# Two of four 768-column differences of token operands made by GpSimd (Pool) instead of VectorE

## The chip, the cores and the metric

One core of a Trainium2 chip runs the whole program. The metric is the time of one execution on the device, in microseconds (us); lower is better. The time of the kernel before is the median of three runs; the profile is that of one execution, which has its own time.

## What is computed

An attention with 32 memory slots, a feed-forward layer with a clipped gate, and a mixture of four experts, all in float32:

```python
a = softmax(phi)                                  # (b, h, s, m), over s
k_m, v_m = a^T k, a^T v                           # 32 memory rows per head
attn_out = softmax(q k_m^T / sqrt(64)) v_m
x = attn_out as (2304, 512)
h = x @ w_in                                      # 2048 columns
x = (h * clip(h + 3, 0, 6) / 6) @ w_out
p = domain_probs / sum(domain_probs)
out = sum over e of p[:, e] * (relu(x @ w1[e]) @ w2[e])   # e = 0..3, 1024 columns each
```

## The kernel before

Every matmul operand is split into a high part (a cast by ScalarE, ACT in the profile) and a low part (a difference by VectorE, DVE), and TensorE (PE) runs three matmuls per product: high by high, high by low, low by high.

**First part.** Attention and the gated layer for 6 token tiles of 384 columns. Their instructions are put in order by a planner at build time (class `Plan`), from written costs and dependences; x^T comes out as the tiles `acc`, one per token tile, as four blocks of 384 columns.

**Second part.** The experts, in 3 passes (p = 0, 1, 2) over pairs of token tiles. A pass has 8 steps n (expert and half of its columns). A step has two units (`unit`), and then the second matmul of the layer (`second`, L953) for both token tiles: 6 blocks of 128 tokens, each added up by DVE into `oacc` (L961, or L959 at the first step of a pass). A unit does a 2 by 2 block product with seven block products instead of eight (L897, banks `pb`, `pa`, `pc`, `pd`): its weight operands `W` are made from `u_raw` by four additions or differences on Pool (`s1`, `s3`, `s2`, `s4`, L326 to L335), a cast on ACT (L320) and a low part on DVE (L323). Products in a unit go b, a, c, d, a, c, d. The second `a` goes into the bank that the first filled, so it waits until DVE has read the first into `u2` (L905, tile `u`), which in turn needs ACT's copy `p6` of bank b (L914, tile `p`).

**The token operands.** The seven blocks that the units multiply by are X11, X21, X22 and T1 to T4. They are made once per pass by `x_ops` (L675) from two `acc` tiles, called B11, B21 (first tile) and B12, B22 (second), each 128 by 768:

- T1 = B12 - B11, written over B11; T3 = B22 - B12, over B12; T2 = B22 - T1, over B22; T4 = B21 - T2, over B21 (the steps `xt1` to `xt4`, L689).
- each of the seven then gets a high part by ACT (`H`, L683) and a low part by DVE (`L`, L686) in its tile `xop`.

T2 is written over B22, which T3 reads: T2 has to come after T3. T4 reads T2.

For p = 0 the planner places the 18 steps among those of the end of the gated layer. For p = 1 and 2 they go into a list `todo` of side work during the last step of the pass before, ahead of what is left of the weight work. `fill(t)` takes from that list until t us of DVE work, by the written costs, are placed: 1.9 us after each block of `second`, 1.2 us after product b of a unit. Steps of ACT and Pool count as nothing in that budget. The first unit of the next pass starts with product b, which takes T2 (first its high part, then its low part), then a (X11), c (T1), d (T3), a (X21), c (X22), d (T4).

Each engine runs its instructions in program order.

Of the kernel before, what the change touches and what calls it, by code (L numbers as in the profile page):

```python
# [13 lines left out]
ALU = mybir.AluOpType  # L14
AX = mybir.AxisListType
PSUM = bass.MemoryType.PSUM

B, H, S, D = 4, 8, 576, 64
M = 32
NT = B * S  # L20
DM = H * D
FF1 = 2048
E, FF2 = 4, 1024
P = 128
# [102 lines left out]
def body(ctx: ExitStack, tc: tile.TileContext, phiT, kv, qT, w_in, w_out, w1, w2, dp, out):  # L127
    nc = tc.nc
# [29 lines left out]
    def bank(name):  # L158
        return ps_w.tile([P, 512], F32, tag="h", name=name)

    plan = Plan()
    op = plan.op
# [262 lines left out]
    def kv_mm(b, c):  # L425
        if c == 0:
            st["pk", b] = [bank("pk")[:, 0:2 * D] for _ in range(2)]
        pk, a, x, n = st["pk", b], st["a", b], st["kv", b, c], SBLK[c][1]
        for hq in range(2):
            for j in range(4):  # L430
                h = 4 * hq + j
                nc.tensor.matmul(pk[hq][M * j:M * j + M], a[:n, c, hq, M * j:M * j + M],  # L432
                                 x[:n, :, h * D:(h + 1) * D], start=(c == 0), stop=(c == 4))

    def kv_out(b, hq):
        if hq == 0:
            st["km", b] = ap_.tile([P, 2, 2 * D], F32, tag="km", name="km")
        nc.scalar.activation(st["km", b][:, hq], st["pk", b][hq], AF.Copy, scale=st["sm", b][:, hq:hq + 1])
# [6 lines left out]
    def kt_out(b, j, r, dst, c0):  # L445
        src = st["pkt", b][r:r + D].rearrange("p q (g o m) -> p (q g) o m", g=2, o=2)[:, :, j]
        nc.scalar.copy(dst[D * j:D * j + D, :, c0:c0 + M], src)

    def sc_size(g):
        return SBLK[GRP[g][-1]][1], len(GRP[g])  # L450

    def sc_mm(b, g):
        ps = st["psc", b, g] = bank("psc").rearrange("p (c h m) -> p c h m", c=2, h=H)
        for j, c in enumerate(GRP[g]):
            s0, n = SBLK[c]
            for hp in range(4):

                nc.tensor.matmul(ps[:n, j].rearrange("p (o g) m -> p g o m", o=2)[:, hp], st["q", b][:, hp, s0:s0 + n],  # L458
                                 kmT[b % 2][:, hp].rearrange("p (o m) -> p o m", o=2), start=True, stop=True)

    def sc_max(b, g):
        n, k = sc_size(g)
        t = st["smx", b, g] = ap_.tile([P, 2, H, 1], F32, tag="smx", name="smx")
        nc.vector.tensor_reduce(out=t[:n, 0:k], in_=st["psc", b, g][:n, 0:k], axis=AX.X, op=ALU.max)

    def sc_sub(b, g):
        n, k = sc_size(g)
        e = st["e", b, g] = ap_.tile([P, 2, H, M], F32, tag="e", name="e", bufs=3)
        nc.vector.tensor_tensor(out=e[:n, 0:k], in0=st["psc", b, g][:n, 0:k],
                                in1=st["smx", b, g][:n, 0:k].to_broadcast([n, k, H, M]), op=ALU.subtract)  # L470

# [193 lines left out]
    X11, X21, X22, XT1, XT2, XT3, XT4 = range(7)  # L665
    xop = {}

    def x_tile(k):
        if k not in xop:
            pool, tag = {X11: (0, "x0"), X21: (0, "x1"), X22: (0, "x2"), XT1: (0, "x3"), XT3: (wip, "wia"),  # L670
                         XT2: (keep_a, "attnT0"), XT4: (keep_a, "attnT1")}[k]
            xop[k] = (pool or late["x"]).tile([P, 2, 2, TW], F32R, tag=tag, name=f"xop{k}")
        return xop[k]

    def x_ops(p):  # L675

        a, b = acc[2 * p] if 2 * p in acc else None, acc.get(2 * p + 1)
        B11, B21 = (lambda: acc[2 * p][:, 0:2]), (lambda: acc[2 * p][:, 2:4])
        B12, B22 = (lambda: acc[2 * p + 1][:, 0:2]), (lambda: acc[2 * p + 1][:, 2:4])
        v = nc.vector.tensor_tensor  # L680

        def hi(k, src):
            nc.scalar.copy(x_tile(k)[:, 0], src())  # L683

        def lo(k, src):
            v(out=x_tile(k)[:, 1], in0=src(), in1=x_tile(k)[:, 0].bitcast(F32), op=ALU.subtract)  # L686

        def sub(out, x, y):
            v(out=out(), in0=x(), in1=y(), op=ALU.subtract)  # L689

        H = lambda k, src: (f"xhi{k}", "A", 750, partial(hi, k, src))
        L = lambda k, src: (f"xlo{k}", "V", 860, partial(lo, k, src))
        D = lambda k, out, x, y: (f"xt{k}", "V", 860, partial(sub, out, x, y))
        return [H(X11, B11), H(X22, B22), H(X21, B21), L(X11, B11), L(X22, B22), D(1, B11, B12, B11),
                D(3, B12, B22, B12), D(2, B22, B22, B11), H(XT2, B22), H(XT1, B11), H(XT3, B12), L(X21, B21),
                L(XT2, B22), L(XT1, B11), D(4, B21, B21, B22), H(XT4, B21), L(XT3, B12), L(XT4, B21)]

    def plan_ffn():
        nu = [(c, b) for c in range(NC1) for b in range(B)]
# [37 lines left out]
        for name, eng, cost, fn in x_ops(0):  # L737
            op((name,), eng, cost, fn, *prev)
            prev = [(name,)]
# [232 lines left out]
    for n in range(last_n + 1):  # L972
        p, c = divmod(n, NCE)
        unit(n, 0)
        unit(n, 1)
        if c == NCE - 1 and p + 1 < NP:
            flush(0)

            at = max([0] + [k + 1 for k, x in enumerate(todo) if x[0] == ("s4", 2 * n + 3)])
            todo[at:at] = [((name, p + 1), cost / 1e3 if eng == "V" else 0, yes, fn) for name, eng, cost, fn in x_ops(p + 1)]  # L980
        second(n, 1)
        second(n, 0)
        if c == NCE - 1 and p + 1 < NP:
            need((f"xlo{XT4}", p + 1))
# [33 lines left out]
```

## Time and profile before

| | us |
|---|---|
| median of 3 runs | 1144.75 (1143.54 to 1149.33) |
| the profiled execution, its own time | 1144.87 |
| its span in the profile | 1143.10 |
| PE busy | 1118.4 |
| DVE busy | 837.9 |
| ACT busy | 462.4 |
| Pool busy | 166.2 |

The span is the profiled stretch; 1.77 us of that execution's own time lie around it. Busy times are sums of what an engine ran, and say nothing yet of what waits for what. Times in the trace count from the start of the span. Two passes end within the second part: the steps for p = 1 lie at about 624 to 657 us, those for p = 2 at about 874 to 906 us, and the last part of the gated layer, with the steps for p = 0, at about 335 to 393 us.

### The profile page before, as it was taken

The page shows a single profiled execution, that of the slowest core. Times are in us where ns is not written, and L with a number is a line of the kernel's source. Part 1 is how long each engine was busy: PE and PEld are TensorE (multiplying, and loading weights), DVE is VectorE, ACT ScalarE, POOL GpSimd, SP SyncE. Part 2 cuts the span into 40 slices and gives each one's busy share as a digit, 9 for nine tenths or more (in the row PEclk, how much of TensorE's full clock was granted, in tenths as well). Part 3 has the DMA queues.
Part 4 walks back from the last instruction along what each step waited for, and adds up shares of the span by engine and source line. Part 5 has one row for each costly group of instructions (what it writes and reads, how often), then busy time and mean ns, then how long its engine had stood idle before and what let it go on. Part 6 is the DMA issues. An engine that isn't in the chain of part 4 may idle for free.

```text
span 1143.1 us, 16606 instructions
## 1 busy us (share of the span) xinstructions
PE 1118.4 (98%) x6488; PEld 1023.3 (90%) x6488; DVE 837.9 (73%) x1510; ACT 462.4 (40%) x918; POOL 166.2 (15%) x200
## 2 busy tenths in 40 slices
PE   4999999999999999999999999999999999999998
PEld 3799999999999989999999899999999899999997
DVE  7999899975558677777666966667777876766664
ACT  3666655433344433333334343333333433333321
POOL 0000000000011022221211322222222122222210
PEclk9899999999999999999999999999999999999999
DMA  9832231210000022221121321222221222221101
GB/s 365 309 107 97 77 109 56 83 48 1 1 19 1 19 91 94 74 75 56 56 72 39 130 93 57 73 74 75 74 74 65 83 77 71 74 75 64 66 1 56
DMA packets 31167, 89.46 MB, mean 78 GB/s; under 512 B 2928, under 2 KB 2928, under 8 KB 30576
## 3 DMA queue, kind: packets, MB, share of 16 engines
q1 hardware_dynamic: 31088, 88.39, 22.5%
q8 instruction: 51, 0.84, 0.3%
q14 instruction: 28, 0.23, 0.1%
HBM read 83.66 MB, written 4.72 MB: 77 GB/s over the span
## 4 chain that ended last, share of the span: by engine, by line
PE 96%; DVE 3%; DMA 0%; ACT 0%; issue 0%; ACTq 0%
PE po L953 34%; PE pacc L648 17%; PE ph L622 9%; PE pa L897 9%; PE pc L897 9%; PE pd L897 8%; PE pb L897 4%; PE psc L458 1%; PE pu L605 1%; PE pk L432 1%; PE pe L503 0%; PE pa L415 0%; DMA raw<-in_w_in 0%; DVE mx L390 0%; DVE cy L230 0%; DVE W L323 0%
## 5 line engine op out<-in xcount | busy, mean ns | idle before, releaser
L953 PE MATMUL po<-w,h 128*128 128x512 f32 x1728 | 396.8, 390 | 0.1
L953 PEld LDWEIGHTS po<-w,h 128*128 128x128 f32 x1728 | 323.9, 188 | 67.0 <-DVE w L355 0.5
L648 PE MATMUL pacc<-g,w 128*128 128x384 f32 x1152 | 213.9, 337 | 0.4 <-DVE g L372 0.4
L648 PEld LDWEIGHTS pacc<-g,w 128*128 128x128 f32 x1152 | 199.0, 188 | 7.7 <-issue 5.9
L961 DVE SCALAR_TENSOR_TENSOR oacc<-po,pr,oacc 128x512 f32<-128x512 f32 x126 | 94.2, 748 | 105.6 <-PE po L953 105.6
L326 POOL TENSOR_TENSOR u_raw<-u_raw 128x256 f32<-128x256 f32 x48 | 37.4, 778 | 923.0 <-DVE pair L323 667.4
L320 ACT CAST W<-u_raw 128x512 fp32r<-128x512 f32 (+1 forms) x160 | 87.4, 600 | 141.7 <-POOL u_raw L329 106.1
L622 PE MATMUL ph<-attnT,u 128*128 128x384 f32 (+1 forms) x768 | 121.2, 306 | 0.1
L897 PE MATMUL pa<-xop,W 128*128 128x384 f32 x576 | 115.5, 334 | 2.8 <-DVE u L905 2.8
L622 PEld LDWEIGHTS ph<-attnT,u 128*128 128x128 f32 x768 | 112.4, 190 | 5.9 <-DVE g L372 1.7
L897 PE MATMUL pc<-xop,W 128*128 128x384 f32 x576 | 115.3, 334 | 0.0
L897 PEld LDWEIGHTS pa<-xop,W 128*128 128x128 f32 x576 | 101.3, 188 | 3.5 <-DVE u L905 3.5
L897 PEld LDWEIGHTS pc<-xop,W 128*128 128x128 f32 x576 | 101.1, 188 | 0.1
L323 DVE TENSOR_TENSOR W<-u_raw,W 128x512 fp32r<-128x512 f32 (+1 forms) x160 | 99.4, 657 | 1.4 <-ACT W L320 0.9
L355 DVE TENSOR_TENSOR w<-w2raw,w 128x512 fp32r<-128x512 f32 x96 | 82.2, 877 | 0.0
L372 DVE TENSOR_TENSOR g<-t,g 128x384 fp32r<-128x384 f32 x96 | 53.3, 557 | 38.2 <-ACT g L369 38.0
L878 ACT ACTIVATE h<-cx 128x384 fp32r<-128x384 f32 x96 | 50.5, 526 | 76.2 <-DVE cx L905 76.2
L369 ACT CAST g<-t 128x384 fp32r<-128x384 f32 x96 | 49.3, 514 | 75.6 <-PE pacc L648 66.8
L914 ACT COPY p<-pb 128x384 f32<-128x384 f32 x48 | 23.0, 480 | 136.9 <-PE pb L897 136.9
L628 ACT ACTIVATE t<-ph,three 128x384 f32<-128x384 f32 x96 | 55.8, 581 | 53.7 <-DVE g L372 44.6
L897 PE MATMUL pd<-xop,W 128*128 128x384 f32 x384 | 76.9, 334 | 0.0
L897 PEld LDWEIGHTS pd<-xop,W 128*128 128x128 f32 x384 | 67.5, 188 | 0.0
(92 smaller groups left out, 1219.6 us busy)
## 6 DMA issues: line engine op xcount, KB each, us to landing
u_raw<-in_w SPq DMA_DIRECT2D x48, 512.0 KB, 3.2
w2raw<-in_w SPq DMA_DIRECT2D x48, 512.0 KB, 3.5
raw<-in_w_in SPq DMA_DIRECT2D x16, 512.0 KB, 4.0
kv<-in_kv SPq DMA_DIRECT2D x16, 512.0 KB, 7.0
raw<-in_w_out SPq DMA_DIRECT2D x16, 512.0 KB, 3.3
q<-in_qT SPq DMA_DIRECT2D x4, 1152.0 KB, 7.6
out_y<-oacc SPq DMA_DIRECT2D x18, 256.0 KB, 2.0
phi<-in_phiT SPq DMA_DIRECT2D x4, 576.0 KB, 8.2
```

The lines of the kernel that those rows point to most:

```text
L320: nc.scalar.copy(w[:, 0], r()[:, slice(*parts[k])])
L323: v(out=W[k][0][:, 1], in0=r()[:, slice(*parts[k])], in1=W[k][0][:, 0].bitcast(F32), op=ALU.subtract)
L355: nc.vector.tensor_tensor(out=w[:, 1], in0=w2raw[n, q // 2][:, q % 2], in1=w[:, 0].bitcast(F32), op=ALU.subtract)
L369: nc.scalar.copy(hi, src)
L372: nc.vector.tensor_tensor(out=lo, in0=src, in1=hi.bitcast(F32), op=ALU.subtract)
L622: nc.tensor.matmul(ps[:, o:o + m], uts[c, b][:, x, hq, i * P:(i + 1) * P], attnT[b][:, y, hq, s0:s0 + m], start=(k == 0), stop=(k == 5))
L628: nc.scalar.activation(t, st["ph", n], AF.Relu, bias=three, scale=1.0)
L648: nc.tensor.matmul(pacc[j][:, 0:TW], w[:, x, j * P:(j + 1) * P], g[:, y], start=(i == 0 and k == 0), stop=(i == NI - 1 and k == 2))
L878: nc.scalar.activation(h[:, 0], src, AF.Relu)
L897: nc.tensor.matmul(bk[b], W[k][0][:, xx, o, kt * P:(kt + 1) * P], xop[x][:, y, kt], start=first and kt == 0 and i == 0, stop=kt == 1 and i ...
L953: nc.tensor.matmul(ps, hts[n, i, half][0][:, x, j * P:(j + 1) * P], w2s[n, i][0][:, y], start=(i == 0 and k == 0), stop=(i == 1 and k == 2))
L961: nc.vector.scalar_tensor_tensor(out=o, in0=ps, scalar=sc, in1=o, op0=ALU.mult, op1=ALU.add)
```

## The change

T3 and T4 become Pool instructions, and the list of 18 steps is written in another order: X21's low part and T1's two parts come between T3 and T2, and T2's two parts around T4. What is computed stays the same.

```diff
+        def sub_pool(out, x, y):
+            nc.gpsimd.tensor_tensor(out=out(), in0=x(), in1=y(), op=ALU.subtract)
+
         H = lambda k, src: (f"xhi{k}", "A", 750, partial(hi, k, src))
         L = lambda k, src: (f"xlo{k}", "V", 860, partial(lo, k, src))
         D = lambda k, out, x, y: (f"xt{k}", "V", 860, partial(sub, out, x, y))
+        G = lambda k, out, x, y: (f"xt{k}", "P", 2300, partial(sub_pool, out, x, y))
         return [H(X11, B11), H(X22, B22), H(X21, B21), L(X11, B11), L(X22, B22), D(1, B11, B12, B11),
-                D(3, B12, B22, B12), D(2, B22, B22, B11), H(XT2, B22), H(XT1, B11), H(XT3, B12), L(X21, B21),
-                L(XT2, B22), L(XT1, B11), D(4, B21, B21, B22), H(XT4, B21), L(XT3, B12), L(XT4, B21)]
+                G(3, B12, B22, B12), L(X21, B21), H(XT1, B11), L(XT1, B11), D(2, B22, B22, B11), H(XT2, B22),
+                G(4, B21, B21, B22), L(XT2, B22), H(XT3, B12), L(XT3, B12), H(XT4, B21), L(XT4, B21)]
```

Lines after L690 are four higher in the changed kernel (L961 becomes L965, L905 becomes L909, L914 becomes L918); the two moved differences are at L692.

**DVE, end of the first pass, before.** `acc_1331` holds B11 and B21, `acc_1555` holds B12 and B22. From the low part of X22 on: T1, T3, an addition of `second`, T2, and the low parts of X21 and T2.

```order
L686 TENSOR_TENSOR xop_3838<-acc_1555,xop_3838 128x768
L689 TENSOR_TENSOR acc_1331<-acc_1555,acc_1331 128x768
L689 TENSOR_TENSOR acc_1555<-acc_1555 128x768
L961 SCALAR_TENSOR_TENSOR oacc_4439<-po,pr,oacc_4439 128x512
L689 TENSOR_TENSOR acc_1555<-acc_1555,acc_1331 128x768
L686 TENSOR_TENSOR xop_3859<-acc_1331,xop_3859 128x768
L686 TENSOR_TENSOR xop_3952<-acc_1555,xop_3952 128x768
```

The same place in the change: T1, the low part of X21, an addition, the low part of T1, T2, the low part of T2, the fourth block's addition.

```order
L686 TENSOR_TENSOR xop_3826<-acc_1555,xop_3826 128x768
L689 TENSOR_TENSOR acc_1331<-acc_1555,acc_1331 128x768
L686 TENSOR_TENSOR xop_3843<-acc_1331,xop_3843 128x768
L965 SCALAR_TENSOR_TENSOR oacc_4439<-po,pr,oacc_4439 128x512
L686 TENSOR_TENSOR xop_3964<-acc_1331,xop_3964 128x768
L689 TENSOR_TENSOR acc_1555<-acc_1555,acc_1331 128x768
L686 TENSOR_TENSOR xop_4042<-acc_1555,xop_4042 128x768
L965 SCALAR_TENSOR_TENSOR oacc_4509<-po,pr,oacc_4509 128x512
```

T3 has left DVE, and T2 stands two low parts later than before, still ahead of the fourth addition.

**Pool, the same place.** The four steps of the weights `u_raw_6185`, then the two moved differences, then the next weights.

```order
 L332 TENSOR_TENSOR u_raw_6185<-u_raw_6185 128x256
 L335 TENSOR_TENSOR u_raw_6185<-u_raw_6185 128x256
+L692 TENSOR_TENSOR acc_1555<-acc_1555 128x768
+L692 TENSOR_TENSOR acc_1331<-acc_1331,acc_1555 128x768
 L326 TENSOR_TENSOR u_raw_6408<-u_raw_6408 128x256
 L329 TENSOR_TENSOR u_raw_6408<-u_raw_6408 128x256
```

T3 stands behind all four steps of `u_raw_6185`, and T4 behind T3.

**DVE, start of the next pass, before.** The fifth addition, T4's low part, the sixth addition, two low parts of `second`'s weights `w`, two low parts `W`, then `u` (this is u2).

```order
L961 SCALAR_TENSOR_TENSOR oacc_4509<-po,pr,oacc_4509 128x512
L686 TENSOR_TENSOR xop_4065<-acc_1331,xop_4065 128x768
L961 SCALAR_TENSOR_TENSOR oacc_4509<-po,pr,oacc_4509 128x512
L355 TENSOR_TENSOR w_8_2_6496<-w2raw_1_6187,w_8_2_6496 128x512
L355 TENSOR_TENSOR w_8_3_6498<-w2raw_1_6187,w_8_3_6498 128x512
L323 TENSOR_TENSOR W_2_6517<-u_raw_6185,W_2_6517 128x512
L323 TENSOR_TENSOR W_1_6519<-u_raw_6185,W_1_6519 128x512
L905 TENSOR_TENSOR u_16_6542<-pa,p_16_6531 128x384
```

And in the change:

```order
L686 TENSOR_TENSOR xop_4092<-acc_1555,xop_4092 128x768
L686 TENSOR_TENSOR xop_4125<-acc_1331,xop_4125 128x768
L965 SCALAR_TENSOR_TENSOR oacc_4509<-po,pr,oacc_4509 128x512
L355 TENSOR_TENSOR w_8_2_6481<-w2raw_1_6187,w_8_2_6481 128x512
L355 TENSOR_TENSOR w_8_3_6483<-w2raw_1_6187,w_8_3_6483 128x512
L965 SCALAR_TENSOR_TENSOR oacc_4509<-po,pr,oacc_4509 128x512
L323 TENSOR_TENSOR W_2_6502<-u_raw_6185,W_2_6502 128x512
L323 TENSOR_TENSOR W_1_6504<-u_raw_6185,W_1_6504 128x512
L323 TENSOR_TENSOR W_0_6506<-u_raw_6408,W_0_6506 128x512
L323 TENSOR_TENSOR pair<-u_raw_6408,pair 128x256
L909 TENSOR_TENSOR u_16_6556<-pa,p_16_6539 128x384
```

Two more low parts of weights (W_0 and `pair`) stand ahead of `u`, since the list of side work is shorter by two DVE steps and the fills reach further into it. The pass from p = 1 to p = 2 has the same rows.

## Rows read from the trace of the kernel before

**Rows 1.** Page, part 1: busy us, share of the span, instructions of each engine

```profile
PE 1118.4 (98%) x6488; PEld 1023.3 (90%) x6488; DVE 837.9 (73%) x1510; ACT 462.4 (40%) x918; POOL 166.2 (15%) x200
```

**Rows 2.** Busy time of each engine by stretch: gated layer's end, two changes of pass

```profile
335.00:392.60 57.60, 57.60 (x368) 55.42 (x367) 41.01 (x71) 26.86 (x50) 4.39 (x4) 1.00 0.00 1
624.30:657.00 32.70, 31.29 (x158) 28.05 (x157) 29.93 (x46) 13.97 (x26) 9.71 (x8) 1.00 0.32 113
873.60:906.30 32.70, 31.29 (x158) 28.07 (x157) 29.96 (x46) 13.97 (x26) 9.73 (x8) 1.00 0.33 113
```

**Rows 3.** The chain that ended last, in order of time: start us, us, what

```profile
593.39 16.36 PE po L953 x72
...
624.34 16.36 PE po L953 x72
...
657.00 16.36 PE po L953 x72
```

**Rows 4.** Timeline of PE at the first change of pass: start, us, instruction, idle before

```profile
640.54 1.23 PE L897 MATMUL pb<-xop,W 128*128 128x384 f32 x6
...
646.30 1.32 PE L897 MATMUL pa<-xop,W 128*128 128x384 f32 x6 [1.41 <-DVE u L905]
```

**Rows 5.** Timeline of DVE, the same stretch

```profile
629.34 0.95 DVE L686 TENSOR_TENSOR xop<-acc,xop 128x768 fp32r<-128x768 f32 x1
...
631.74 0.95 DVE L689 TENSOR_TENSOR acc<-acc,acc 128x768 f32<-128x768 f32 x1
632.72 1.38 DVE L689 TENSOR_TENSOR acc<-acc 128x768 f32<-128x768 f32 x1
...
634.69 0.94 DVE L689 TENSOR_TENSOR acc<-acc,acc 128x768 f32<-128x768 f32 x1
635.55 2.36 DVE L686 TENSOR_TENSOR xop<-acc,xop 128x768 fp32r<-128x768 f32 x2
...
639.36 0.95 DVE L689 TENSOR_TENSOR acc<-acc,acc 128x768 f32<-128x768 f32 x1
...
642.63 0.74 DVE L961 SCALAR_TENSOR_TENSOR oacc<-po,pr,oacc 128x512 f32<-128x512 f32 x1
643.29 1.28 DVE L355 TENSOR_TENSOR w<-w2raw,w 128x512 fp32r<-128x512 f32 x2
644.49 1.28 DVE L323 TENSOR_TENSOR W<-u_raw,W 128x512 fp32r<-128x512 f32 x2
645.69 0.55 DVE L905 TENSOR_TENSOR u<-pa,p 128x384 f32<-128x384 f32 x1
...
650.90 0.42 DVE L323 TENSOR_TENSOR pair<-u_raw,pair 128x256 fp32r<-128x256 f32 x1
```

**Rows 6.** Timeline of Pool, the same stretch

```profile
629.56 1.33 POOL L326 TENSOR_TENSOR u_raw<-u_raw 128x256 f32<-128x256 f32 x1 [21.52 <-DVE W L323]
630.97 2.32 POOL L329 TENSOR_TENSOR u_raw<-u_raw 128x256 f32<-128x256 f32 x1
633.37 1.34 POOL L332 TENSOR_TENSOR u_raw<-u_raw 128x256 f32<-128x256 f32 x1
634.79 1.44 POOL L335 TENSOR_TENSOR u_raw<-u_raw 128x256 f32<-128x256 f32 x1
```

**Rows 7.** The line L326, whole span: durations ns, min/median/max

```profile
L326 POOL TENSOR_TENSOR u_raw<-u_raw x48: 732/737/1382, 323.3 to 1097.2; 128x256 f32<-128x256 f32 x48
```

**Rows 8.** Groups of Pool instructions by line: count, busy us, mean ns

```profile
L1011 POOL MEMSET const-float32-0.0<- 128x1 f32 x1 | 0.1, 98 | 0.2 <-issue 0.2
```

**Rows 9.** Timeline of ACT, the first change of pass

```profile
635.66 2.31 ACT L683 CAST xop<-acc 128x768 fp32r<-128x768 f32 x3 [7.98 <-DVE acc L689]
640.40 0.84 ACT L683 CAST xop<-acc 128x768 fp32r<-128x768 f32 x1 [2.43 <-DVE acc L689]
641.14 1.14 ACT L351 CAST w<-w2raw 128x512 fp32r<-128x512 f32 x2
...
644.05 0.47 ACT L914 COPY p<-pb 128x384 f32<-128x384 f32 x1
```

## The prediction, made before the changed kernel ran

> **What bounds the kernel now.** I read first the page's busy times: PE is busy for 1118.4 of 1143.1 us, DVE for 838 and Pool for 166 [rows 1]. So DVE's work as such is no bound; only what PE waits for counts. The table by stretch says where that is. At the end of the gated layer, where the steps for p = 0 lie, PE is busy for all of 57.60 us, and DVE for 41.01. In both changes of pass PE is busy for 31.29 of 32.70 us [rows 2]: 1.41 us of waiting each, the same in both. The chain of waits puts a price on it: a step of the second part takes 624.34 - 593.39 = 30.95 us, the one over the change of pass 657.00 - 624.34 = 32.66, so 1.71 us more [rows 3]. That is 1.41 us of waiting and 0.3 of taking up again. All that the change could ever win is therefore 2 x 1.71 = 3.4 us, or 0.3%; a measurement of this kernel can tell about 0.5% (5.7 us) from no change.
>
> The wait itself is in PE's timeline: the second product a starts at 646.30 after 1.41 us idle, released by DVE's `u` (u2) [rows 4]. DVE's timeline says why u2 is late: from 629.34 to 645.69 its instructions follow one another without idle time, and u2 stands behind all of them [rows 5]. ACT's copy p6, which u2 also needs, is done at 644.05 + 0.47 = 644.52 and is not the last [rows 9].
>
> **How Pool and DVE meet.** Pool's steps on 256 columns have a median of 737 ns [rows 7], but the four in the change of pass take 1.33, 2.32, 1.34 and 1.44 us [rows 6]: they wait while DVE runs differences with both inputs in SBUF. It goes the other way too. The difference T3 of DVE starts at 632.72 and takes 1.38 us instead of 0.95, since Pool's second step is under way until 630.97 + 2.32 = 633.29; DVE ends at 634.10, 0.81 after Pool [rows 5, 6]. So the two exclude each other, and the later one waits for the other's end.
>
> **The change, part by part.**
>
> *Removed from DVE.* T3 and T4, 0.95 us each alone, with the next instruction starting 0.86 after the start (634.69 to 635.55) [rows 5]. This is 1.7 us per pass, and in a change of pass DVE is what PE waits for.
>
> *Added to Pool.* Two steps of 768 columns. The trace has none that long. A Pool instruction on one column takes 98 ns [rows 8], so 256 columns cost (737 - 98)/256 = 2.5 ns each, and 768 make 0.098 + 1.92 = 2.02 us. Upper bound: three times 0.737 = 2.21. Lower bound: 0.737 and 512 columns at DVE's pace, (0.95 - 0.42)/512 = 1.04 ns each [rows 5], so 1.27. I take 2.02, as Pool's own rows are the nearest. Pool is idle enough for it; its place in the queue is what matters.
>
> *T3 at a change of pass.* In Pool's queue it stands behind four steps of weights. These start at 629.56 and end at 634.79 + 1.44 = 636.23 [rows 6]; in the change DVE runs as many two-input differences beside them (X11, X22, T1, X21, T1's low part), so I keep that end. T3 then runs from 636.31 to 638.33. DVE comes to T2 at 631.74 + 3 x 0.86 + 0.66 = 635.0 (T1, two low parts, an addition; [rows 5]), with one hold about 635.5, and must wait, since T2 overwrites what T3 reads: T2 runs from 638.43 to 639.38. It ran at 634.69 before [rows 5]. Behind the waiting T2 in DVE's queue stand the low part of T2 and the fourth addition, which is ready from 624.34 + 4 x 16.36/6 = 635.25 on [rows 3]; all of it slips. **This wait is the new thing, and 2.9 us of DVE's time go into it.**
>
> *T4 and the low part of T2.* T4 needs T2 and so starts on Pool at about 639.46 and ends at 641.48. ACT casts T2 until about 640.3 (0.84 for one [rows 9]). Its low part could then start, but Pool holds it until 641.48; it ends 0.81 later, at 642.29. Product b of the next pass, which starts at 640.54 to 640.70 [rows 3, 4], takes the low part with its second matmul. PE waits there for about 1.4 us, where it waited for nothing before: T2's low part used to end at 637.91 [rows 5].
>
> *The queue up to u2.* After the low part of T2 DVE's next start is 642.21. Then, by the spacing of starts: three additions at 0.66 (642.63 to 643.29), the low parts of T3 and T4 at 0.86, two of `w` and two of `W` at 0.60 (643.29 to 645.69 for four) [rows 5], and the two that the fills have moved ahead of u2, W_0 at 0.60 and `pair` at 0.33 (0.42 less the overlap of 0.09). The sum is 1.98 + 1.72 + 2.40 + 0.93 = 7.03. So u2 starts at 649.24 instead of 645.69, 3.55 us later. ACT's chain after T4 (T4's high part, six casts, p6) takes until about 646 and does not decide. PE's second a follows u2 as before, at 649.85 instead of 646.30. Between the two waits PE has a, c and d to do, 3.1 us from 643.2, so it runs dry again at 646.3.
>
> *Per change of pass* that makes 3.55 us, and there are two: +7.1.
>
> *End of the gated layer (p = 0).* Here Pool has T3 ahead of four weight steps, and T2 stands behind some ten other DVE instructions, so T2 finds T3 done. T3 and T4 each may hold one of DVE's two-input differences for up to 2.02 us; DVE gives up 1.7 us of its own and has 16.6 us free in 57.6 [rows 2]. The operands are wanted only at 392.6. I cost it at nothing; without that cover it is up to 2 x 2.02 = 4.0 us. Loads: no DMA is added, and a load that waits for a raw buffer behind `W_1` starts some 3 us later, with about as long until its use; nothing.
>
> **Sum:** the profiled execution took 1144.87 us (its span is 1143.10; that execution is 0.12 above the median of 1144.75). 1144.87 + 7.1 = **1152.0 us**, 0.6% slower.
>
> **A rule of the skill.** The trace shows holds of DVE of 0.43 us [rows 5], with Pool instructions of 0.74 us. The Trainium skill, page "SBUF — State Buffer", section "Who interferes with whom", says that a DVE instruction with two SBUF inputs contends with a GpSimd instruction that reads SBUF, and that whoever comes first has the port pair for its whole instruction. By that rule T4 holds the low part of T2 to its end, as in the sum (+7.1); were a hold never longer than 0.43, it would start at 640.73 and u2 come 0.75 earlier, +5.6 in all. No run here shows a Pool instruction of 768 columns yet.
>
> **Rivals.**
> 1. *Shorter Pool steps or a shorter hold.* At 1.27 us T3 ends at 637.58, T2 at 638.63, T4 at 639.98, T2's low part at 640.79: u2 comes 2.05 later, +4.1 in all, 1149.0. With the short hold alone it is 1150.5. For it: nobody has timed such a step here. Against: Pool's own pace, 2.5 ns per column. Chance 0.20.
> 2. *The gated layer pays as well.* One or two holds of 2.02 us fall on a low part of `g` that PE wants at once: 1154 to 1156. For it: PE has no idle time there, so a late `g` costs at once. Against: DVE's slack. Chance 0.12.
> 3. *Not slower: Pool keeps ahead.* If the weight steps on Pool end early enough that T3 is done when DVE comes to T2 at 635.5, DVE has 1.72 less to do ahead of u2 and 0.93 more, and T2's low part is in time. u2 then starts 0.8 earlier and PE waits 0.6 instead of 1.41: 1144.87 - 1.6 = 1143.3. It decides at 633.4, the time by which the four steps have to be done (2.02 and a gap of 0.08 before 635.5). For it: alone they would take about 3 us from 629.56. Against: they took until 636.23, and DVE's queue beside them is as dense as it was [rows 5, 6]. Chance 0.07.
>
> That the steps don't move is no rival: Pool's order has them.
>
> **How the numbers follow.** The forecast has 0.61, the rivals 0.20, 0.12 and 0.07. The range leaves out rival 3, the lowest part of rival 1 and what lies above rival 2: 1147.5 to 1156.0. Its upper end also takes Pool steps of 2.21 us (+0.76). Slower by over 0.5% means above 1150.5: nearly all of the forecast (0.55) and rival 2, together 0.67. Within 0.5%: rivals 1 and 3 and the rest of the forecast, less 0.02, so 0.31. Faster by over 0.5% is 0.02, since only 3.4 us of waits are there to be won.
>
> **What would show it.** In the changed profile: Pool's L692 at about 2.0 us; DVE idle for 2 to 3 us ahead of T2 in both changes of pass, released by Pool; a wait of PE in product b on the low part of T2, and a longer one at the second a; a step over the change of pass of 36 us instead of 32.66; no idle time of PE between 335 and 393 us. Wrong would be: T3 ending before DVE is at T2, Pool steps near 1 us, or waits of PE in the gated layer.

## The result and the profile after

| | us |
|---|---|
| before, median of 6 runs | 1146.56 (1143.54 to 1149.33) |
| the change, median of 6 runs | 1155.35 (1154.17 to 1159.49) |
| ratio, 95% interval | 1.0076 [1.0056, 1.0096] |
| the change's profiled execution, its own time | 1156.2 |
| its span | 1154.4 (before: 1143.10) |

The change made the kernel 0.76% slower. The page of the changed kernel shows where the work went: DVE has six instructions less and Pool six more, and Pool is busy 11.5 us longer [rows 1]:

```profile
PE 1123.6 (97%) x6488; PEld 1027.0 (89%) x6488; DVE 836.2 (72%) x1504; ACT 463.3 (40%) x918; POOL 177.7 (15%) x206
```

PE runs the same 6488 matmuls, yet is busy 5.2 us longer, 3.7 of it in the two changes of pass (33.32 and 32.91 us there, 31.25 and 31.26 before). That is the first sign of something the prediction did not have.

**Where the 11.3 us of span come from.** The chain of waits of the changed kernel, in order of time (start us, us, what), answers to [rows 3]:

```profile
341.81 5.94 PE pacc L648 x33
...
410.38 15.07 PE po L957 x65
...
625.71 2.78 PE po L957 x12
...
637.87 1.80 POOL acc L692
640.83 1.82 POOL acc L692
644.03 1.62 DVE xop L686 x2
648.37 1.80 DVE W L323 x3
651.03 1.33 PE pa L901 x6
652.38 2.05 PE pc L901 x6
654.43 1.86 PE pd L901 x6
...
663.58 16.36 PE po L957 x72
...
880.21 2.78 PE po L957 x12
...
905.53 2.29 PE pa L901 x6
907.82 1.50 PE pc L901 x6
917.64 16.36 PE po L957 x72
```

Two Pool instructions of the token operands now stand on the chain. The step over the first change of pass is 663.58 - 625.71 = 37.87 us, where it was 32.66: +5.21. The second is 917.64 - 880.21 = 37.43: +4.77. Together +9.98. The other +1.37 is already there at the first of them (625.71 against 624.34), and 1.14 of it before either of the moved differences has run once (the first starts at 355.40): a row of the gated layer starts at 341.81 in the chain of the change and at 340.67 in that of before:

```profile
340.67 5.94 PE pacc L648 x33
...
409.04 15.03 PE po L953 x65
```

This 1.14 is not the change's. From that row to the first `second` it is 68.57 us in the change and 68.37 before, so 0.20 of the 1.37 comes in the gated layer; E4 comes back to it. Executions of one and the same kernel differ by some 7 us (before: 1143.5 to 1150.7 over all comparisons), and the profiled ones differ at their beginning: over the first 50 us PE's granted clock was 0.93 in that of before and 0.90 in this one. Steps of the chain are therefore the sharper measure here, and the experiments are read by them.

**Inside a change of pass.** PE's timeline (start, us, instruction, idle time before):

```profile
641.91 0.33 PE L901 MATMUL pb<-xop,W 128*128 128x384 f32 x1
643.50 1.14 PE L901 MATMUL pb<-xop,W 128*128 128x384 f32 x5 [1.26 <-DVE xop L686]
...
646.56 1.21 PE L901 MATMUL pd<-xop,W 128*128 128x384 f32 x6
651.03 1.33 PE L901 MATMUL pa<-xop,W 128*128 128x384 f32 x6 [3.26 <-DVE u L909]
652.38 2.05 PE L901 MATMUL pc<-xop,W 128*128 128x384 f32 x6
654.23 2.07 PE L901 MATMUL pd<-xop,pair 128*128 128x384 f32 x6
656.13 1.21 PE L901 MATMUL pb<-xop,W 128*128 128x384 f32 x6
```

There are two things to see. First the waits: 1.26 us in product b on T2's low part, 3.26 at the second a on u2, where there was one wait of 1.41 [rows 4]. The second a starts 651.03 - 625.71 = 25.32 us into the step, and started 646.30 - 624.34 = 21.96 into it before: +3.36. Then the two products behind the long wait: c and d take 2.05 and 2.07 us, where a product with nothing in its way takes 1.2. The table by stretch (stretch; its length, then busy time of PE, PEld, DVE, ACT, Pool; PE's granted clock; DMA share; GB/s) has the reason in the column after Pool's; its first two rows are the beginning and the end of the gated layer, of which the text speaks elsewhere:

```profile
0.00:50.00 50.00, 32.26 (x325) 25.11 (x325) 40.54 (x91) 24.67 (x56) 1.20 (x8) 0.90 0.93 343
...
335.00:392.60 57.60, 57.60 (x368) 55.19 (x367) 39.79 (x69) 28.17 (x51) 7.73 (x6) 1.00 0.01 1
...
652.00:654.00 2.00, 1.98 (x9) 1.65 (x8) 1.31 (x3) 0.91 (x2) 1.84 (x3) 0.67 0.77 253
654.00:656.00 2.00, 2.00 (x8) 2.00 (x7) 1.49 (x3) 0.53 (x1) 0.08 (x1) 0.50 0.04 12
656.00:658.00 2.00, 2.00 (x13) 2.00 (x12) 1.62 (x3) 1.08 (x3) 0.00 (x0) 0.97 0.00 0
```

The clock was 1.00 in every stretch shown of before [rows 2]. Here it falls to 0.50, which is 1.2 GHz instead of 2.4, for some 3 us, and PE does the same matmuls slower. From the second a to the end of the step it is 663.58 - 651.03 = 12.55 us instead of 657.00 - 646.30 = 10.70: +1.85. So 5.21 = 3.36 up to the second a + 1.85 behind it. At the second change of pass it is 3.36 and 1.41. Not all that lies behind it is the clock's: E9 below splits it.

**Why the waits are there** is in DVE's timeline and Pool's. DVE, one row of the gated layer, and then from the instruction ahead of T2 to u2 and the next `u` (`u<-pc`), which the second product c waits for:

```profile
355.70 2.34 DVE L323 TENSOR_TENSOR W<-u_raw,W 128x512 fp32r<-128x512 f32 x1
...
635.51 0.95 DVE L686 TENSOR_TENSOR xop<-acc,xop 128x768 fp32r<-128x768 f32 x1
639.69 0.96 DVE L689 TENSOR_TENSOR acc<-acc,acc 128x768 f32<-128x768 f32 x1 [3.23 <-POOL acc L692]
641.56 1.89 DVE L686 TENSOR_TENSOR xop<-acc,xop 128x768 fp32r<-128x768 f32 x1 [0.91 <-ACT xop L683]
...
650.43 0.55 DVE L909 TENSOR_TENSOR u<-pa,p 128x384 f32<-128x384 f32 x1
650.90 0.97 DVE L355 TENSOR_TENSOR w<-w2raw,w 128x512 fp32r<-128x512 f32 x1
651.79 0.54 DVE L909 TENSOR_TENSOR u<-pc,u 128x384 f32<-128x384 f32 x1
```

Pool, the same stretch:

```profile
632.34 3.19 POOL L329 TENSOR_TENSOR u_raw<-u_raw 128x256 f32<-128x256 f32 x1
635.61 1.44 POOL L332 TENSOR_TENSOR u_raw<-u_raw 128x256 f32<-128x256 f32 x1
637.13 0.74 POOL L335 TENSOR_TENSOR u_raw<-u_raw 128x256 f32<-128x256 f32 x1
637.82 1.83 POOL L692 TENSOR_TENSOR acc<-acc 128x768 f32<-128x768 f32 x1
640.79 1.84 POOL L692 TENSOR_TENSOR acc<-acc,acc 128x768 f32<-128x768 f32 x1 [1.14 <-DVE acc L689]
```

T2 stands idle in DVE's queue for 3.23 us until T3 is done on Pool, which itself waited behind the four weight steps. Then T2's low part takes 1.89 us instead of 0.95, since T4 is under way on Pool until 642.63; it ends 0.82 us after that.

### The profile page after: what moved, and what is told of

Its sections match the earlier page's. It is cut to its first block, busy times and chain, and to the rows that moved or that the text cites. A ratio compares the mean times of both kernels' runs of the same rounds, so it can differ in the third digit from the quotient of the medians.

```text
span 1154.4 us, 16608 instructions
## 1 busy us (share of the span) xinstructions
PE 1123.6 (97%) x6488; PEld 1027.0 (89%) x6488; DVE 836.2 (72%) x1504; ACT 463.3 (40%) x918; POOL 177.7 (15%) x206
## 4 chain that ended last, share of the span: by engine, by line
PE 93%; DVE 4%; POOL 2%; ACT 1%; issue 0%; DMA 0%; POOLq 0%; DVEq 0%; ACTq 0%
PE po L957 32%; PE pacc L648 17%; PE ph L622 10%; PE pa L901 9%; PE pc L901 9%; PE pd L901 8%; PE pb L901 4%; PE psc L458 1%; PE pu L605 1%; PE pk L432 1%; POOL acc L692 1%; POOL u_raw L329 1%; DVE W L323 1%; PE pe L503 0%; DVE oacc L965 0%
## 5 line engine op out<-in xcount | busy, mean ns | idle before, releaser
L648 PE MATMUL pacc<-g,w 128*128 128x384 f32 x1152 | 214.0, 337 | 0.4 <-DVE g L372 0.4
L648 PEld LDWEIGHTS pacc<-g,w 128*128 128x128 f32 x1152 | 198.9, 188 | 7.7 <-issue 5.9
L326 POOL TENSOR_TENSOR u_raw<-u_raw 128x256 f32<-128x256 f32 x48 | 36.7, 764 | 887.7 <-DVE pair L323 670.4
L965 DVE SCALAR_TENSOR_TENSOR oacc<-po,pr,oacc 128x512 f32<-128x512 f32 x126 | 94.3, 748 | 105.4 <-PE po L957 105.4
L918 ACT COPY p<-pb 128x384 f32<-128x384 f32 x48 | 23.1, 481 | 141.8 <-PE pb L901 141.8
## 6 DMA issues: line engine op xcount, KB each, us to landing
q<-in_qT SPq DMA_DIRECT2D x4, 1152.0 KB, 7.7
```

Of the source, the lines that this page charges most:

```text
L648: nc.tensor.matmul(pacc[j][:, 0:TW], w[:, x, j * P:(j + 1) * P], g[:, y], start=(i == 0 and k == 0), stop=(i == NI - 1 and k == 2))
L965: nc.vector.scalar_tensor_tensor(out=o, in0=ps, scalar=sc, in1=o, op0=ALU.mult, op1=ALU.add)
```

## The experiments

Steps are those over the two changes of pass, from the start of one `second` to the start of the next, in us of the profiled execution. Times are medians; the ratio compares the runs with those of the kernel before on the same chip and is not the quotient of two medians. The median of before was 1146.27 beside E1 to E4, 1145.89 beside E5 to E8 and 1146.89 beside E9 and E10.

| kernel | steps | median | ratio, 95% interval |
|---|---|---|---|
| before | 32.66, 32.67 | | 1 |
| the change | 37.87, 37.43 | 1155.35 | 1.0076 [1.0056, 1.0096] |
| E1 new order, all on DVE | 32.67, 32.66 | 1146.35 | 0.9996 [0.9979, 1.0013] |
| E2 only T4 on Pool | 33.09, 33.10 | 1150.26 | 1.0033 [1.0017, 1.0048] |
| E3 only T3 on Pool | 34.14, 34.14 | 1150.42 | 1.0027 [1.0006, 1.0048] |
| E4 gated layer as before | 37.58, 38.58 | 1154.4 | 1.0085 [1.0056, 1.0114] |
| E5 T3 and T4 ahead of the weight steps | 36.56, 36.34 | 1156.82 | 1.0066 [1.0040, 1.0092] |
| E6 before, u2 earlier | 31.53, 31.53 | 1143.46 | 0.9969 [0.9951, 0.9988] |
| E7 the change, u2 earlier | 33.87, 33.89 | 1149.98 | 1.0017 [0.9998, 1.0035] |
| E8 E5 and E7 together | 33.44, 33.41 | 1150.97 | 1.0024 [1.0005, 1.0043] |
| E9 the change, two idle products | 36.30, 36.31 | 1155.33 | 1.0083 [1.0058, 1.0108] |
| E10 before, one idle product | 32.67, 32.67 | 1149.0 | 1.0006 [0.9988, 1.0025] |

The theory was the prediction's: T2 waits for T3 on Pool, T2's low part is held by T4, and u2 stands behind both. The rivals were the order of the list by itself, and the gated layer.

**E1: the new order, with T3 and T4 on DVE in the second part.**

```diff
+        S3 = G if p == 0 else D
+        S4 = G if p == 0 else D
-                G(3, B12, B22, B12), L(X21, B21), ...
+                S3(3, B12, B22, B12), L(X21, B21), ...
-                G(4, B21, B21, B22), L(XT2, B22), ...
+                S4(4, B21, B21, B22), L(XT2, B22), ...
```

> For p = 1 and 2 the steps stand in the changed order, but all four differences are DVE's; p = 0 is as in the change. My theory (T2 waits for Pool's T3, then T4 holds the low part of T2): both waits are gone, DVE has again the two differences ahead of u2 and the fills end where they ended before. The step over a change of pass is 32.5 to 33.0 us (before 32.66, changed 37.9 and 37.4), PE's clock stays at full speed there, the time is 1144 to 1147 us. Rival (the new order alone makes T2's parts too late): the step stays above 36 us and the time near 1154.

The steps are those of the kernel before, 32.67 and 32.66. In the changes of pass the order of the list costs nothing; it is Pool that costs. This kernel still has T3 and T4 of the gated layer on Pool.

**E2: only T4 on Pool** (S3 as above, T4 stays on Pool).

> For p = 1 and 2 T3 is DVE's again, T4 stays on Pool. My theory: T2 waits for nothing on Pool; T4 starts when T2 ends and still holds the low part of T2 for about 1 us, which DVE gets back by not making T4. u2 starts 0.2 to 0.6 us later than before, the step over a change of pass is 32.7 to 33.3 us, the time 1145 to 1147. Rival (each Pool step costs its half): the step is 35 us, the time 1150.

**E3: only T3 on Pool** (S4 as above, T3 stays on Pool).

> For p = 1 and 2 T3 stays on Pool, T4 is DVE's again. My theory: DVE idles about 3 us ahead of T2 as in the change; T4 and an addition now stand ahead of the low part of T2, which comes about 0.8 us after PE wants it; u2 starts 1.2 to 1.6 us later than before. The step over a change of pass is 33.9 to 34.3 us at full clock, up to 36 where the clock falls after the wait as it did in the change; the time is 1148 to 1152. Rival (T4's hold is the main cost): no more than 33 us, and a DVE wait ahead of T2 that costs nothing.

T4 alone adds 0.43, T3 alone 1.48; both steps came as expected. E2's median, 1150.26, was expected at 1145 to 1147 and stands higher than two steps of +0.43 would put it. Its profiled execution had a granted clock of 0.83 in the first 50 us, and its first `second` starts at 413.83, so in that execution this part is the beginning's and not T4's. The lowest of its ten executions, 1144.61, is 1.12 above the lowest of before, 1143.49; but eight of the ten lie above 1149, and 7 of the 26 of before. Why more of them were long is not shown. E3 has the wait at T2 by itself, as its DVE timeline shows:

```profile
635.77 0.95 DVE L686 TENSOR_TENSOR xop<-acc,xop 128x768 fp32r<-128x768 f32 x1
639.95 1.95 DVE L689 TENSOR_TENSOR acc<-acc,acc 128x768 f32<-128x768 f32 x2 [3.23 <-POOL acc L692]
```

It is the same 3.23 us as in the change, but costs only 1.48 here. DVE makes T4 itself and holds its own place, T2's low part is not held, and the fills do not reach as far ahead of u2. Alone the two cost 1.91 together, side by side 3.36 by the waits alone. In E3 PE waits 0.98 and 1.67 us, and its clock stays at 1.00.

**E4: the gated layer with the old list**, the second part as in the change.

```diff
+        if p == 0:
+            return [... D(3, B12, B22, B12), D(2, B22, B22, B11), ... the list of before ...]
```

> p = 0 as before the change (order and engines), p = 1 and 2 as in the change. My theory: the gated layer's end pays nothing in either form, so the steps over the changes of pass are 37 to 38 us and the time is within 1 us of the change's. Rival (the holds in the gated layer cost too): 1 to 4 us less than the change.

The time is that of the change, and so is the first step. The second, 38.58, is 1.15 longer than the change's and above what was expected; its waits are the same, 1.26 and 3.26 us, and the difference lies behind the second a. The medians, 1154.4 and 1155.35, cannot tell a cost of 1 us. The chains can: from the row of the gated layer named above to the first `second` E4 takes 413.72 - 345.34 = 68.38 us, like the kernel before (68.37), and the change takes 68.57, like E1 (68.55). So the gated layer pays 0.2 us for its new list, and nearly the whole loss is in the changes of pass. The planner also puts PE's matmuls there in another order (the next run of L648 behind that row has 9 matmuls instead of 3), so whether the 0.2 comes from Pool or from that order is not shown.

**E5: T3 and T4 ahead of the four weight steps in Pool's queue**, by putting the 18 steps into the list of side work before `s1` instead of after `s4`.

```diff
-            at = max([0] + [k + 1 for k, x in enumerate(todo) if x[0] == ("s4", 2 * n + 3)])
+            at = max([0] + [k for k, x in enumerate(todo) if x[0] == ("s1", 2 * n + 3)])
```

> As the change, but at a change of pass the token steps go into the list ahead of Pool's four weight steps, so that Pool takes T3 right after T1 and the weight steps after T4. My theory (T2 waits because T3 stands behind the weight steps): DVE's wait ahead of T2 falls from 3.2 to under 1 us, product b finds the low part of T2 in time. The weight steps then meet the low parts behind it and may hold them by up to 0.6 us each. u2 starts 1.1 to 3.5 us later than before the change: the step over a change of pass is 33.8 to 36.2 us (changed 37.9 and 37.4), PE's clock is less likely to fall, the time is 1147 to 1152 us. Rival (two Pool steps of 1.8 us cost DVE that much wherever they stand): the step stays at 37 us or more.

The steps, 36.56 and 36.34, and the median lie above what was expected. The wait at T2 is gone, and so is the one in product b. But DVE lost nearly as much in another way. From its timeline:

```profile
634.23 1.94 DVE L686 TENSOR_TENSOR xop<-acc,xop 128x768 fp32r<-128x768 f32 x1
636.09 0.94 DVE L689 TENSOR_TENSOR acc<-acc,acc 128x768 f32<-128x768 f32 x1
637.94 1.91 DVE L686 TENSOR_TENSOR xop<-acc,xop 128x768 fp32r<-128x768 f32 x1 [0.90 <-ACT xop L683]
...
640.43 2.35 DVE L686 TENSOR_TENSOR xop<-acc,xop 128x768 fp32r<-128x768 f32 x2
...
643.37 1.82 DVE L355 TENSOR_TENSOR w<-w2raw,w 128x512 fp32r<-128x512 f32 x2
```

Undisturbed these take 0.95, 0.95, 1.81 and 1.28 us, so Pool held DVE for 0.99 + 0.96 + 0.54 + 0.54 = 3.03 us. In the kernel before the same reckoning gives 0.98 (T3, and two low parts in 2.36) [rows 5]. T3 and T4 save DVE 1.7 us and cost it 2 in holds and 0.9 in idle time, and W_0 and `pair` still stand ahead of u2 (0.93 by the prediction's reckoning): together 2.1, and the second a starts 648.51 - 624.43 = 24.08 us into the step instead of 21.96. Neither of the two places in Pool's queue that were tried wins. PE then has one wait of 3.53 us ahead of the second a, and the clock falls behind it again, where the other 1.78 of the +3.90 lies: 0.93, 0.50 and 0.72 in the stretches 648:650 to 652:654.

**E6: the kernel before, with u2 earlier.** In the first unit of a pass the 1.2 us of side work after product b (two low parts `W`, which no product needs so soon) go behind u2.

```diff
-        step(1.2)
+        first = u == 0 and n % NCE == 0 and n > 0
+        step(0 if first else 1.2)
...
         h_tile(n, u + 2, 1, add_to(c_tile("cy"), "d", tmp["u4"]))
-        step(0)
+        step(0.6 if first else 0)
         prod("a", 0, 1, X21, False, True)
         h_tile(n, u, 0, bk["a"])
-        step(0)
+        step(0.6 if first else 0)
```

> The kernel before, with one thing changed: in the first unit of a pass the side work that stood ahead of u2 (two low parts of weights, 1.2 us) goes behind it. It tests the reading that the queue of DVE ahead of u2 is what PE waits for. My theory: u2 starts when p6 is there, about 1.1 us earlier, the step over a change of pass is 31.4 to 31.9 us (before 32.66), the time 2 us less: ratio to before 0.997 to 0.999. Rival (p6 or something else is as late): the step stays at 32.6 us.

**E7: the change, with the same edit**, and no fill after the last block ahead of the new pass.

```diff
-            fill(1.9)
+            fill(0 if c == NCE - 1 and half == 0 and j == 2 else 1.9)
```

> The change, with the four low parts of weights that stand ahead of u2 (2.1 us) put behind it; T3 and T4 stay on Pool and where they were. My theory: the wait ahead of T2 (3.2 us) and PE's wait in product b (1.26) stay as they are; u2 starts 2.1 us earlier, so PE's wait at the second a falls from 3.26 to about 1.1; with 2.4 us of waits PE's clock stays up, as it did with 2.65 us in the run with T3 alone on Pool. The step is 33.5 to 34.0 us at full clock (35.7 if it falls), the time 1147 to 1149. Rival (T3's wait is paid in full whatever stands behind it): 36 us or more.

**E8: E5 and E7 together.**

> The change with both: the token steps ahead of Pool's weight steps, and the low parts of weights behind u2. My theory: with T3 early and the queue ahead of u2 short, u2 starts between 1 us earlier and 1.4 us later than before the change (holds by the weight steps decide), the step is 31.4 to 34 us, the time 1142 to 1148: at best 2 us under the kernel before. Rival (Pool's steps cost DVE as much as they save wherever they stand): the step is above 34 us.

E6 takes 1.13 us off each step and is faster than both kernels. What PE waits for at the second a is left in its timeline with 0.28 us:

```profile
643.94 1.32 PE L897 MATMUL pa<-xop,W 128*128 128x384 f32 x6 [0.28 <-DVE u L905]
```

E7 has its wait at the second a in PE's timeline, and E8 what its u2 waits for in DVE's:

```profile
647.41 1.31 PE L901 MATMUL pa<-xop,W 128*128 128x384 f32 x6 [1.12 <-DVE u L909]
```

```profile
650.66 0.56 DVE L909 TENSOR_TENSOR u<-pa,p 128x384 f32<-128x384 f32 x1 [0.68 <-ACT p L918]
```

In E7 the wait at T2 is still 3.23 us and T2's low part still takes 1.89, yet the steps are 4.0 and 3.5 us shorter than the change's: the last wait falls by 2.14, to 1.12, and what lay behind it, 1.85 and 1.41, is gone, with the clock at 1.00. Part of this the kernel before can have as well, as E6 shows. Against E6 the steps of E7 are still 2.34 and 2.36 longer: that is what T3 and T4 on Pool cost where the queue ahead of u2 is short. In E8 PE waits 2.17 us at the second a, and there u2 waits for ACT's copy p6, which stands behind casts of weights that come late from Pool. The steps of both lie in the expected ranges, the medians (1149.98 and 1150.97) above them. No version with T3 and T4 on Pool is faster than the kernel before; all are slower than E6.

**E9: is it the clock?** That the 1.85 us behind the long wait are the clock's was so far read from one column. This run adds 12 matmuls to the change: product b twice over into its own bank, after ACT has copied it, between product d and the second a. Their results are not used.

```diff
+        if u == 0 and n % NCE == 0 and n > 0:
+            for r in range(2):
+                for kt in range(2):
+                    for i, (xx, y) in enumerate(PASSES):
+                        nc.tensor.matmul(bk["b"], W[1][0][:, xx, 0, kt * P:(kt + 1) * P], xop[XT2][:, y, kt],
+                                         start=kt == 0 and i == 0, stop=kt == 1 and i == 2)
```

> The change with 12 matmuls more in the first unit of a new pass, between product d and the second a: product b is made twice over again into its bank, after ACT has copied it, and never read, so nothing that is computed changes. They lie in PE's wait of 3.26 us. Theory (the lower granted clock behind the long wait costs 1.8 and about 1.4 us of the two changes of pass): PE has 2.1 us to do in the wait, about 1.1 us of it is left, second a still starts about 25.3 us after the step's start, the granted clock stays at 1.00 behind it, and the two steps are 36.0 to 36.2 us instead of 37.87 and 37.43, though PE does more. Rival (the slow products c and d after the wait have another cause, such as waits for operands or transfers beside them): the steps stay at 37.4 to 37.9, or grow.

**E10: the control**, one such product in the kernel before.

> Control: the kernel before with one more product b (6 matmuls, never read) at the same place. PE's wait ahead of second a shrinks from 1.41 to about 0.3 us, second a starts as before, and the steps stay at 32.66 us (32.6 to 32.8), since the clock was at 1.00 behind the wait of 1.41 anyway. If an extra product costs time of its own there, or filling a wait gains something else than the clock, the steps differ from 32.66 by over 0.2.

E9's timeline of PE:

```profile
646.80 1.20 PE L901 MATMUL pd<-xop,W 128*128 128x384 f32 x6
647.84 2.24 PE L935 MATMUL pb<-xop,W 128*128 128x384 f32 x12
651.27 1.32 PE L901 MATMUL pa<-xop,W 128*128 128x384 f32 x6 [1.18 <-DVE u L909]
652.62 1.31 PE L901 MATMUL pc<-xop,W 128*128 128x384 f32 x6
653.77 1.20 PE L901 MATMUL pd<-xop,pair 128*128 128x384 f32 x6
```

The second a starts 25.32 us into the step (651.27 - 625.95), to the hundredth as in the change: DVE is as late as ever. But c and d now take 1.31 and 1.20 us, the table by stretch has a clock of 1.00 there, and the steps are 36.30 and 36.31, that is 1.57 and 1.12 shorter than the change's, though PE does 12 matmuls more in each:

```profile
652.00:654.00 2.00, 1.96 (x12) 1.64 (x11) 1.30 (x4) 0.73 (x2) 1.84 (x3) 1.00 0.87 306
654.00:656.00 2.00, 2.00 (x13) 2.00 (x12) 2.00 (x4) 0.70 (x2) 0.33 (x1) 1.00 0.02 7
```

It is 0.1 above what was expected, as product c still starts late (1.35 us after the second a, before 1.15): it waits for `u<-pc`, which in DVE's queue stands behind a low part of `w`, as in the change. From the second a to the end of the step E9 takes 662.25 - 651.27 = 10.98 us at full clock, 0.28 more than before. So of the 1.85 and 1.41 us in the change 0.28 each is there without the clock's fall, and 1.57 and 1.12 are the clock's. The DMA share in 652:654 is 0.87, more than the change's 0.77, so transfers were not what slowed c and d. The control's steps stay at 32.67: where the clock does not fall, such products neither cost nor gain. So the fall of the clock is shown as the cause of that part. The median does not tell E9 from the change (1155.33 of four runs); a difference of 2.7 us is too small for it, beside executions of one kernel that differ by 5 and more.

## Why the prediction was right, and which term it lacked

The forecast was 1152.0 us, 7.1 more than before; measured were 8.8 more by the medians, and 9.98 by the two steps. The direction, the place and the mechanism of the delay up to the second a were right. That 1155.35 lies in the range is in part luck: the part of the range above 1154 was there for holds in the gated layer (rival 2), which did not come; what filled it is what the sum lacked behind the second a. Times of the change are given here less 1.37, by which its step starts later.

- **Pool's price.** 2.02 us was taken for 768 columns, and 1.83 and 1.84 were measured. The estimate from 2.5 ns per column [rows 7, 8] was 0.19 too long: from 0.737 us at 256 columns to 1.835 at 768 it is 2.14 ns per column, which leaves a fixed part of 0.19 us and not the 98 ns of the one-column instruction. It made little difference, since T3's end (638.28, forecast 638.33) also depends on when the weight steps end: 636.50, forecast 636.23.
- **The wait at T2.** 2.9 us expected, 3.23 measured; T2 starts at 638.32, forecast 638.43. E3 shows this wait by itself, E5 shows that Pool's queue order makes it.
- **T4 against T2's low part.** Forecast was an end at 642.29, 0.81 after Pool's; it was 642.08, 0.82 after. The Trainium skill, page "SBUF — State Buffer", section "Who interferes with whom", has the second engine blocked for the first one's whole instruction. The trace agrees: the low part took 1.89 us instead of 0.95 beside a Pool step of 1.84, more than the 0.43 us of hold that the trace of before could show [rows 5]. The rival with a short hold and shorter Pool steps falls with that. (Its price for the short hold, u2 0.75 earlier, goes by T4's end; by the prediction's own end of the low part it is 642.21 - (640.73 + 0.86) = 0.62, so +5.9 in all and not +5.6.)
- **Product b and u2.** The wait in b was to be 1.4 and is 1.26; u2 was to start at 649.24 and starts at 649.06, the second a at 649.85 and starts at 649.66. So the delay per change of pass was forecast as +3.55 and is +3.36.
- **The gated layer.** Costed at nothing; by the chains of E4 and the change it is 0.2 us. In its stretch PE is still busy all the time, and DVE gives up 1.2 us: the stretch 335:392.6 of the table above, beside its row of before [rows 2].

- **Pool keeps ahead** (the rival that ends not slower): it was to decide at 633.4, and the weight steps ended at 636.50. Nothing of it happened. Pool's second weight step even took 3.19 us instead of 2.32 [rows 6], as DVE ran three differences one after another, until 634.93; the step ended 0.60 behind them, at 635.53, so most of its 0.74 us came after the third.
- **The step that failed** is "*Per change of pass* that makes 3.55 us": it takes the delay of the second a as the whole cost, with every product behind it as fast as before. The products behind it took 1.85 and 1.41 us longer: PE's granted clock fell to 0.50 after the wait of 3.26 us, which is 1.57 and 1.12 of it by E9, and product c waited for DVE, 0.28 each. With the measured 3.36 instead of 3.55 the two steps would make +6.7; with what lies behind the second a they make +9.98. The second part of the trace of before shows no such fall, and its longest wait there is 1.41 us, but the table by stretch has the column, and a forecast that lengthens PE's waits should give it a term.

## What to carry to other kernels

Two engines that exclude each other are not two engines: a difference moved from DVE to Pool holds DVE's own differences while it runs, and a step that is written in place makes DVE wait for Pool's whole queue ahead of it. Before moving work off a busy engine, look at what stands in its queue ahead of the one instruction that the bottleneck waits for; 1.2 us of side work that nobody needed yet was worth more here (E6) than two whole instructions on another engine. A long wait of PE can cost more than its length, so read the granted clock behind the wait too.

## What the runs showed of the hardware that was not expected

- **The clock behind a wait.** It stayed at 1.00 behind waits of 1.41 (before), 0.98 and 1.67 (E3), 1.26 and 1.12 (E7) and 2.17 us (E8). It fell to 0.50 behind 1.26 and 3.26 (the change, E4) and behind a single wait of 3.53 (E5). The cost differs from one to the next: 1.57 and 1.12 us in the change, while E4's second step, with the same waits, is 1.15 longer than the change's. What decides between the two groups was not tried and stays open.
- **Twelve matmuls for nothing made a step shorter** by 1.57 and 1.12 us (E9).
- **The beginning differs from execution to execution.** Over the first 50 us the granted clock was 0.97 in E6's profile, 0.93 before, 0.90 in the change and 0.83 in E2, and the first `second` started at 407.82, 409.04, 410.38 and 413.83. Why it differs was not looked into.

- **A longer Pool step holds DVE longer, in the gated layer too.** Beside T3 of the gated layer a low part `W` on DVE took 2.34 us (the first row of DVE's timeline above), where two undisturbed ones take 1.28 [rows 5]; PE stayed busy in that stretch.
